# Two spectral filters and a gate: sums of the last four inverse rows on TensorE, and a new order of work

## The chip, the cores and the metric

One core of a Trainium2 chip runs the whole kernel. The metric is the device time of one execution in microseconds (us), as the median of several runs. The profile is of one execution; its span, from the first to the last instruction of the program, is a little shorter than the device time of that same execution.

## The reference

```python
# x: 2048 x 1024 (bf16), w_r, w_i: 2048 x 513 for each of A and B, gate_w: 1024
g = sigmoid((x * gate_w).sum(-1, keepdims=True))
a = irfft2(rfft2(x) * (A_w_r + 1j * A_w_i))      # over both axes, then bf16
b = irfft2(rfft2(x) * (B_w_r + 1j * B_w_i))
out = g * a + (1 - g) * b
```

Only `A_x` is used. The Fourier transforms run over the 2048 rows (s) and the 1024 columns (d) of one image.

## The kernel before

Row s = 16p + n of x lies on partition p, so the image is 16 slabs n of 128 x 1024. The work runs in stages, each a set of small tasks; a task is one entry of a list.

1. **Forward s, first radix** (`fold`, `fod`, `s1.n.t`, `evz`; n = 0 to 7 stands for a pair of slabs, t = 0 for the even and 1 for the odd columns of the d spectrum). VectorE (DVE) first folds x: sums (t = 0) or differences (t = 1) of the two halves of d, in two instructions `fold n.t.0` and `fold n.t.1`, the second of which reads backwards, so that the result lies folded for the next step. For t = 0 two further instructions `fod n.0.k` form sums and differences of that once more. Then TensorE (PE) multiplies with the cosines and sines in FM (eight 256-column matmuls for one `s1`), whose negatives `neg0` to `neg3` ScalarE (ACT) makes in FM's upper half. A `raw` task (FOLD0) leaves out the two `fod` and makes PE do their sums, in longer matmuls; a FOLD2 task does the opposite for t = 1. Each result goes from PSUM to SBUF (R3) through one eviction `evz`, on ACT or DVE.
2. **Forward d** (`d0` to `d15`, `evq`): eight matmuls each, four 128-column ones that read the t = 0 results and four 256-column ones that read t = 1; every `d` waits for all sixteen `evz`. The evictions write the RING buffer; `qc` copies two columns out for the Nyquist column.
3. **Forward s, second radix** (`s2.j.c`, `evx`), **product** with A's and B's weights (`p b.j.t`, on DVE, optionally followed by `ps`, which adds the two halves so that PE needs half the matmuls: SUMS), **inverse s** (`i b.T`, `evv`). The Nyquist column goes apart: `x5` on PE, `x5e`, then `p5.b` on GpSimd (POOL), `v5.b` on PE, `v5e.b`, and a small DMA `vf b` that needs all `evv b.*` and `v5e.b`. TensorE's list places `v5.0` and `v5.1` between the `i` tasks.
4. **Inverse d** (`dinv b.n`, `evd`; 32 of them). A `dinv0` needs all of V of filter A and `vf0`, a `dinv1` all of B and `vf1`.
5. **Inverse s, last step with the gate** (`s1i m`, m = 0 to 15, `evo`): four 512-column matmuls, weighted with RA and RB, which hold the gated cosines. The evicted cosine and sine sums are then unfolded on DVE in three steps of two instructions each: `q a/b`, `h a/b`, `y a/b`, for two slabs at a time (the last two slabs alone), and `out n` on SyncE's DMA queue (SP) writes the result. The gate's own path is `gj`, `g8`, `g9` (POOL), `grow`, `gzr`, `gzt`, `gzg`, `gmix`, `sig`, `ra`, `rb`.

The order of work is written out by hand: `ORDER` is a list of `task:engine+buffers`, `place` assigns engine and buffer from it, and each engine's instructions run in exactly that order. `:p0` to `:p3` is the PSUM slot (four of 1024 fp32 columns), `:a` ACT, `:d` DVE, `:g` POOL, `:s` SP. DMAs are all issued by SP, in list order, so a load that has to wait holds up those behind it. The loads of weights (`w b.t.c.pm`, 128 KB in each of two DMAs, mostly) keep three in flight: each waits until the third before it has landed.

All engines record through helpers, so that the profile's lines are those of helpers: L421 is the matmul, L424 a DVE or POOL tensor_tensor, L428 the ACT eviction, L429 the DVE eviction, L444 the loads and L1018 the stores. The profile names tiles without numbers: R stands for R1 to R5.

Of the kernel before, what the change touches and what calls it, by code (L numbers as in the profile page):

```python
# [6 lines left out]
ALU = mybir.AluOpType  # L7
# [14 lines left out]
mz:g x2:s x12:s table:a warm:p0 F:s x0:s x14:s x8:s x4:s w0.0.0.0:s fold1.0.0:d0 fold1.0.1:d0 fold1.1.0:d1 RM:s  # L22
fold1.1.1:d1 DM:s fold6.0.0:d2 fod1.1.1:d fod1.1.0:d fold6.0.1:d2 w0.0.1.0:s fold6.1.0:d3 fod1.0.0:d neg0:a
fold6.1.1:d3 neg1:a w0.0.0.1:s fod1.0.1:d fod6.1.0:d fod6.1.1:d s1.1.1:p1 fod6.0.0:d neg3:a fod6.0.1:d fold0.1.1:d1
s1.6.1:p2 evz1.1:a fold0.0.0:d0 SK:s fold0.0.1:d0 s1.1.0:p3 fold0.1.0:d1 neg2:a fod0.0.1:d fod0.0.0:d fold7.1.0:d3
fod0.1.1:d fod0.1.0:d evz6.1:a fold7.1.1:d3 s1.6.0:p0 fold7.0.0:d2 fold7.0.1:d2 s1.0.0:p1 fod7.1.0:d evz6.0:a
fod7.1.1:d fold4.0.0:d4 evz1.0:a fold4.1.1:d5 s1.7.1:p2 fold4.1.0:d5 evz0.0:a s1.0.1:p0 fold4.0.1:d4 fod4.1.1:d
fod4.1.0:d fod5.1.1:d fod5.1.0:d s1.4.1:p3 fold2.1.0:d0 evz0.1:a fold2.1.1:d0 s1.5.1:p1 evz4.1:a fod4.0.0:d fod3.1.0:d
fod3.1.1:d fod2.1.0:d fod2.1.1:d w0.0.1.1:s s1.3.1:p0 fold2.0.0:d3 evz5.1:a fod4.0.1:d s1.2.1:p3 evz7.1:a fod7.0.1:d
fod7.0.0:d s1.5.0:p1 fold2.0.1:d3 evz2.1:a s1.4.0:p2 fod2.0.0:d evz5.0:a fod2.0.1:d s1.7.0:p3 w0.4.0.1:s evz4.0:a  # L30
evz3.1:d s1.2.0:p1 evz7.0:a w0.4.0.0:s s1.3.0:p2 evz2.0:d evz3.0:a w0.4.1.0:s d7:p00 d2:p31 evq7:d w0.8.0.0:s d3:p11
evq2:a d6:p20 evq3:d w0.4.1.1:s d1:p02 evq6:a d0:p32 evq1:d qc1:a qc3:a w0.8.0.1:s s2.3.1:p1 evq0:a s2.3.0:p2 evx3.1:d
s2.1.1:p0 GW:s evx3.0:a s2.1.0:p3 w0.8.1.1:s evx1.1:d evx1.0:a d4:p10 d5:p20 w0.8.1.0:s evq4:a p0.3.1:d0 d10:p31
evq5:a p0.3.0:d0 s2.0.0:p0 w0.12.0.0:s ps0.3.1:d d11:p11 evq10:a qc2:d evx0.0:d s2.2.1:p2 ps0.3.0:d evq11:a s2.0.1:p3
evx2.1:d evx0.1:a s2.2.0:p0 s2.5.1:p1 qc0:a p0.0.0:d1 evx5.1:a i0.6:p3 i0.7:p2 evx2.0:d evv0.6:a w0.12.1.0:s ps0.0.0:d
s2.5.0:p1 evv0.7:a p0.0.1:d1 gj:p3 d12:p00 w0.12.0.1:s evx5.0:a d8:p22 qc5:d g8:d ps0.0.1:d p0.1.1:d0 g9:g d13:p30
evq12:a w0.12.1.1:s i0.0:p1 p0.1.0:d0 evq13:a ps0.1.1:d i0.1:p0 w1.0.0.1:s evq8:a evv0.0:d ps0.1.0:d s2.6.1:p3
evv0.1:a s2.6.0:p2 qc6:d p0.2.1:d1 w1.0.0.0:s d14:p11 evx6.1:a d9:p02 p0.2.0:d1 GS:s evx6.0:a w1.0.1.0:s i0.2:p3
evq9:a ps0.2.1:d d15:p21 w1.4.0.0:s ps0.2.0:d evq14:a evv0.2:d i0.3:p0 evq15:a w1.0.1.1:s i0.5:p1 p0.5.0:d0 i0.4:p3
evv0.3:a s2.7.0:p2 qc4:d evv0.4:a p0.6.0:d1 w1.4.0.1:s ps0.5.0:d grow:p0 evv0.5:a qc7:d p0.6.1:d1 ps0.6.0:d w1.4.1.1:s  # L40
evx7.0:a s2.7.1:p3 gzr:d s2.4.1:p1 ps0.6.1:d evx7.1:a w1.4.1.0:s s2.4.0:p2 p0.5.1:d0 gzt:p0 evx4.1:a DI:s i0.12:p3
p0.7.0:d2 ps0.5.1:d evx4.0:a w1.8.0.0:s i0.13:p1 gzg:d evv0.12:a p0.7.1:d2 ps0.7.0:d x5:p2 i0.10:p0 x5e:a evv0.13:a
p0.4.1:d1 p5.0:g ps0.7.1:d i0.11:p3 w1.8.0.1:s evv0.10:a p0.4.0:d1 ps0.4.1:d gmix0:p2 evv0.11:a w1.8.1.0:s gmix1:p1
p1.0.0:d0 ps0.4.0:d i0.15:p0 sig0:a w1.8.1.1:s i0.14:p3 p1.0.1:d0 sig1:a ps1.0.0:d i0.8:p2 evv0.15:a p1.2.1:d2
ps1.0.1:d w1.12.0.0:s v5.0:p1 evv0.14:a p1.2.0:d2 i0.9:p0 ps1.2.1:d evv0.8:a w1.12.0.1:s i1.0:p3 p1.1.0:d1 ps1.2.0:d
v5e.0:a i1.1:p2 w1.12.1.0:s evv0.9:a p1.1.1:d1 ps1.1.0:d i1.4:p1 evv1.1:a w1.12.1.1:s p1.5.1:d0 ps1.1.1:d i1.5:p0
evv1.0:a vf0:s p1.5.0:d0 i1.2:p2 ps1.5.1:d evv1.4:a i1.3:p3 p1.4.1:d2 evv1.2:a ps1.5.0:d i1.11:p1 evv1.5:a p1.4.0:d2
ps1.4.1:d i1.10:p2 evv1.3:a p5.1:g p1.6.1:d1 ps1.4.0:d i1.9:p0 evv1.11:a p1.6.0:d1 i1.8:p3 ps1.6.1:d evv1.10:a
dinv0.7:p1 p1.7.0:d0 evv1.9:a ps1.6.0:d dinv0.10:p2 evd0.7:a p1.7.1:d0 dinv0.8:p0 ps1.7.0:d evv1.8:a i1.13:p1
p1.3.0:d2 ps1.7.1:d evd0.10:a i1.12:p3 p1.3.1:d2 evv1.13:a i1.14:p2 ps1.3.0:d evd0.8:a i1.15:p1 ps1.3.1:d evv1.12:a  # L50
evv1.14:d i1.7:p0 evv1.15:a i1.6:p3 evv1.7:d v5.1:p2 evv1.6:a dinv0.12:p1 v5e.1:d dinv0.2:p0 evd0.12:a ra1:d
dinv0.0:p3 vf1:s dinv0.11:p2 rb1:d evd0.0:a evd0.2:d dinv0.6:p1 evd0.11:a dinv0.9:p3 evd0.6:d dinv0.15:p0 evd0.9:a
dinv1.8:p2 evd0.15:d dinv1.9:p1 evd1.8:a dinv1.7:p3 ra0:d evd1.9:a dinv1.6:p0 rb0:d s1i8:p20 evd1.7:d evd1.6:a
s1i9:p10 evo8.0:d dinv1.3:p0 evo9.0:a dinv1.15:p3 evd1.3:a q8a:d dinv1.11:p2 q8b:d s1i6:p11 evd1.15:a h8a:d0 h8b:d0
dinv1.10:p0 evd1.11:a s1i7:p31 y8b:d0 evd1.10:a evo6.0:d s1i15:p22 evo7.0:a dinv1.1:p0 y8a:d0 evo15.0:a q6b:d
s1i10:p13 evd1.1:a evo15.1:d dinv1.2:p3 q6a:d evo10.0:a q15a:d q15b:d dinv1.0:p2 h6b:d1 evd1.2:a s1i11:p03 h6a:d1
h15a:d0 evd1.0:a dinv1.13:p1 y6a:d1 dinv0.13:p3 y6b:d1 evo11.0:a dinv1.12:p2 evd1.13:d evd0.13:a dinv0.1:p0 q10a:d
# [249 lines left out]
class Task:  # L307
# [3 lines left out]
    n = 0  # L311
# [57 lines left out]
def build(nc, A_x, A_w_r, A_w_i, B_w_r, B_w_i, gate_w, out):  # L369
# [154 lines left out]
    for c in range(4):  # L524
        t = add(f"neg{c}", -1500 + c, {"act": (0.48, 0.6)}, None, [tF, tb])
        t.emit = lambda g, c=c: S.op("act", [lambda e: e.activation(ap(FM, 2048 + c * 512, [[1, 512]]), ap(FM, c * 512, [[1, 512]]),  # L526
                                                                  ACT.Copy, scale=-1.0)], ["F"], [("FN", c)])
        tN.append(t)
# [6 lines left out]
    allZ, evZ = [], []  # L535
    for Q in range(4):
        for t in range(2):

            st = Buf("st")
            folds, part = {}, {}  # L540
            for n0, n1 in (((0, 1), (1, 2)) if Q in (0, 3) else ((0, 2),)):
                fs = []
                for hv in range(2):
                    f = add(f"fold{2 * Q + n0}.{t}.{hv}", -900 + 2 * Q + n0, tt_cost(512 * (n1 - n0)), None,
                            [xt[2 * Q + i] for i in range(n0, n1)], [st])

                    def e_f(g, Q=Q, t=t, n0=n0, n1=n1, hv=hv, st=st):
                        nn, so = 2 * (n1 - n0), (4 * Q + 2 * n0) * 1024
                        o = st.i * 2048 + n0 * 1024
                        if t:  # L550
                            d = [[1024, nn], [-1 if hv else 1, 256]]
                            w, lo = ap(RING, o + hv * 256, [[512, nn], [1, 256]]), 511 * hv
                        else:
                            d = [[1024, nn], [-256, 2], [-1, 128]] if hv else [[1024, nn], [256, 2], [1, 128]]
                            w = ap(RING, o + 128 * hv, [[512, nn], [128 if hv else 384, 2], [1, 128]])
                            lo = 511 * hv
                        S.op(g, [tt(w, ap(R1, so + lo, d), ap(R1, so + 512 + lo, d), ALU.subtract if t else ALU.add)],
                             [("x", 2 * Q + i) for i in range(n0, n1)], [("st", st.i, i, hv) for i in range(n0, n1)])
                    f.emit = e_f
                    fs.append(f)  # L560
                if not t:
                    gs = []
                    for k in range(2):
                        f = add(f"fod{2 * Q + n0}.0.{k}", -900 + 2 * Q + n0, tt_cost(512 * (n1 - n0)), None, fs, [], [st])
# [12 lines left out]
                for i in range(n0, n1):  # L577
                    folds[i], part[i] = fs, n0
            for i in range(2):
# [18 lines left out]
                if not t:  # L598
                    u.alt = ("G", Q, part[i], {0: (pe_cost(872), 16), 1: (pe_cost(1735), 20)})
# [450 lines left out]
```

## Time and profile before

| | |
|---|---|
| device time, median of 11 runs | 128.88 us (126.47 to 131.11) |
| profiled execution, device time | 128.24 us |
| its span | 126.1 us |
| granted TensorE clock, mean | 0.974 |
| busy in the span: DVE / PE / ACT / POOL | 111.1 / 109.9 / 105.5 / 16.6 us |
| read from memory, written | 14.77 MB, 4.19 MB |

Instruction durations overlap: a DVE eviction of 128 x 1024 takes 1.22 us, but two in a row start 1.13 us apart. For sums of work the distance from start to start (the step) is what counts, and it is read from rows in which several of a kind follow without a gap. The tasks of the list appear in each engine's trace in list order, so that every DVE, ACT and PE instruction can be given its task's name by counting.

### The profile page before, as it was taken

The page shows a single profiled execution, that of the slowest core. Times are in us where ns is not written, and L with a number is a line of the kernel's source. Part 1 is how long each engine was busy: PE and PEld are TensorE (multiplying, and loading weights), DVE is VectorE, ACT ScalarE, POOL GpSimd, SP SyncE. Part 2 cuts the span into 40 slices and gives each one's busy share as a digit, 9 for nine tenths or more (in the row PEclk, how much of TensorE's full clock was granted, in tenths as well). Part 3 has the DMA queues.
Part 4 walks back from the last instruction along what each step waited for, and adds up shares of the span by engine and source line. Part 5 has one row for each costly group of instructions (what it writes and reads, how often), then busy time and mean ns, then how long its engine had stood idle before and what let it go on. Part 6 is the DMA issues. An engine that isn't in the chain of part 4 may idle for free.

```text
span 126.1 us, 4191 instructions
## 1 busy us (share of the span) xinstructions
PE 109.9 (87%) x1853; PEld 82.0 (65%) x1853; DVE 111.1 (88%) x163; ACT 105.5 (84%) x120; POOL 16.6 (13%) x22
## 2 busy tenths in 40 slices
PE   5999999699999999999499999999999999976000
PEld 2367878586468785699399889899666766631000
DVE  0699799499999999999769999999899999999940
ACT  4078999389999999999869999998799999999200
POOL 2000000000005800049749000000000000000000
PEclk9999999999999999999999999999999999999955
DMA  4999999889955759759610000000000000402997
GB/s 112 407 430 426 297 311 247 166 222 173 191 136 172 209 153 247 219 149 229 183 58 7 5 5 0 5 1 5 0 0 0 5 0 0 166 0 86 402 404 273
DMA packets 13425, 19.23 MB, mean 153 GB/s; under 512 B 2656, under 2 KB 10848, under 8 KB 13152
## 3 DMA queue, kind: packets, MB, share of 16 engines
q1 hardware_dynamic: 13408, 18.98, 49.7%
q8 instruction: 14, 0.23, 0.8%
q14 instruction: 3, 0.02, 0.0%
HBM read 14.77 MB, written 4.19 MB: 150 GB/s over the span
## 4 chain that ended last, share of the span: by engine, by line
ACT 42%; PE 19%; DVE 13%; DMA 9%; POOL 6%; issue 3%; SPq 2%; ACTq 1%; DVEq 1%
ACT R L428 34%; PE PS L421 19%; DVE RING L424 12%; DMA R<-in_A_x_dram 9%; ACT RING L428 8%; POOL P L424 6%; SPq L444 2%; DVE R L424 1%; ACTq L285 1%; DVEq L285 0%; DVEq L271 0%; ACT X L428 0%
## 5 line engine op out<-in xcount | busy, mean ns | idle before, releaser
L428 ACT ACTIVATE R<-PS 128x1024 bf16<-128x1024 f32 (+1 forms) x94 | 87.5, 1092 | 4.0 <-PE PS L421 3.5
L424 DVE TENSOR_TENSOR RING<-R 128x2048 bf16<-128x2048 bf16 (+2 forms) x74 | 59.1, 846 | 7.2 <-DMA R<-in_A_x_dram 4.9
L421 PE MATMUL PS<-DM,R 128*128 128x256 bf16 (+1 forms) x384 | 34.4, 246 | 1.2 <-ACT R L428 1.1
L421 PEld LDWEIGHTS PS<-DM,R 128*128 128x128 bf16 x384 | 28.5, 98 | 7.1 <-ACT R L428 1.8
L421 PE MATMUL PS<-SK,RING 64*128 64x128 bf16 x960 | 29.2, 217 | 0.3 <-issue 0.2
L421 PEld LDWEIGHTS PS<-SK,RING 64*128 64x128 bf16 x960 | 27.1, 102 | 2.3 <-issue 1.0
L429 DVE CAST R<-PS 128x1024 bf16<-128x1024 f32 (+1 forms) x20 | 23.4, 1190 | 0.1
L424 DVE TENSOR_TENSOR R<-R 128x512 bf16<-128x512 bf16 (+2 forms) x36 | 16.5, 508 | 1.0 <-ACT R L428 0.8
L421 PE MATMUL PS<-R,FM 128*128 128x512 bf16 x64 | 15.4, 379 | 0.9 <-ACT R L428 0.8
L428 ACT ACTIVATE RING<-PS 128x1024 bf16<-128x1024 f32 x13 | 12.6, 1055 | 1.9 <-PE PS L421 1.9
L421 PEld LDWEIGHTS PS<-R,FM 128*128 128x128 bf16 x64 | 6.0, 98 | 7.4 <-ACT R L428 2.0
L421 PE MATMUL PS<-FM,RING 128*128 128x256 bf16 (+1 forms) x66 | 8.7, 283 | 0.2 <-DVE RING L424 0.2
L424 POOL TENSOR_TENSOR P<-X,R 128x32 bf16<-128x32 bf16 x4 | 6.9, 1732 | 13.7 <-ACT X L428 11.5
L421 PE MATMUL PS<-RING,SK 64*64 64x512 bf16 (+1 forms) x128 | 8.6, 384 | 0.1
L421 PEld LDWEIGHTS PS<-FM,RING 128*128 128x128 bf16 x66 | 6.2, 98 | 2.4 <-ACT FM L526 0.6
L424 POOL TENSOR_TENSOR GW<-GW 128x8 bf16<-128x8 bf16 (+1 forms) x4 | 2.5, 666 | 38.0 <-DVE GW L429 38.0
L421 PE MATMUL PS<-R 128*128 128x512 bf16 x16 | 6.4, 588 | 1.3 <-POOL R L514 1.3
L421 PE MATMUL PS<-FM,R 128*128 128x256 bf16 (+1 forms) x64 | 7.1, 266 | 0.0
L421 PEld LDWEIGHTS PS<-FM,R 128*128 128x128 bf16 x64 | 5.9, 98 | 0.9 <-DVE R L424 0.2
L526 ACT ACTIVATE FM<-FM 128x512 bf16<-128x512 bf16 x4 | 2.3, 620 | 4.6 <-DMA FM<-c_F 4.6
L424 DVE TENSOR_TENSOR R<-RING 128x512 bf16<-128x512 bf16 (+1 forms) x12 | 5.6, 506 | 0.0
L421 PEld LDWEIGHTS PS<-R 128*128 128x128 bf16 x16 | 2.2, 143 | 5.0 <-issue 3.6
(35 smaller groups left out, 36.0 us busy)
## 6 DMA issues: line engine op xcount, KB each, us to landing
out_dram<-RING SPq DMA_DIRECT2D x7, 512.0 KB, 4.3
R<-in_A_x_dram SPq DMA_DIRECT2D x4, 512.0 KB, 5.2
R<-in_A_x_dram SPq DMA_DIRECT2D x2, 1024.0 KB, 10.1
R<-in_A_w_r_dram SPq DMA_DIRECT2D x15, 128.2 KB, 3.8
R<-in_A_w_i_dram SPq DMA_DIRECT2D x15, 128.2 KB, 3.7
R<-in_B_w_r_dram SPq DMA_DIRECT2D x15, 128.2 KB, 3.2
R<-in_B_w_i_dram SPq DMA_DIRECT2D x15, 128.2 KB, 2.8
FM<-c_F SPq DMA_DIRECT2D x1, 512.0 KB, 5.2
```

What stands on the lines that cost most here:

```text
L285: with nc.Block() as block:
L421: return lambda e: e.matmul(o, l, r, start=start, stop=stop, skip_group_check=True)
L424: return lambda e: e.tensor_tensor(out=o, in0=a, in1=b, op=op)
L428: return lambda e: e.activation(o, i, ACT.Copy)
L429: return lambda e: e.tensor_copy(o, i)
L444: t.emit = lambda g: S.op(eng, [lambda e, d=d, s=s: e.dma_start(d, s, **kw) for d, s in pairs], reads, writes, dma=kind, after=after)
L526: t.emit = lambda g, c=c: S.op("act", [lambda e: e.activation(ap(FM, 2048 + c * 512, [[1, 512]]), ap(FM, c * 512, [[1, 512]]), ACT.Copy, s ...
```

## The change

- **Last four rows.** LATE = 4: for m = 12 to 15 PE forms, besides each 512-column matmul, the folded second half with two 256-column matmuls more (12 instead of 4 matmuls in a task), using negated copies of RA and RB (`nr0`, `nr1`, 512 columns each, into RM). For these rows DVE does `q` and `y` only; their `h` are gone.
- **Folds in one instruction.** For t = 0 the two half-length folds become one full-length instruction (`fold n.0.2`) that leaves the result unfolded, and `fod` reads its second operand backwards. The raw task moves from n = 0 to n = 7; FOLD2 is empty, so `s1.7.1` is an ordinary one and its two `fod` are gone. `ps` is used for three j (A: 3 and 5, B: 6) in place of two.
- **Forward d in two parts.** `d g.0` holds the four 128-column matmuls and waits for the t = 0 evictions, `d g.1` the four 256-column ones and waits for t = 1; one eviction serves both.
- **A new list.** `neg3` and `nr0` go to DVE as tensor_scalar. Of the evictions, DVE takes 2 `evz`, 5 `evq`, 3 `evx`, 3 `evv`, 8 `evd`, 1 `evo` (before: 2, 3, 5, 4, 6, and two and a half `evo`), and all eight `qc`.

The list by engine, where the text below needs it:

```
SP   x12 F x14 x2 x0 x8 x4 w0.0.0.1 DM w0.0.0.0 GW SK w0.0.1.0 w0.0.1.1 ... w1.4.1.0 RM w1.8.0.0 w1.8.0.1
     w1.4.1.1 w1.8.1.1 w1.12.0.0 w1.8.1.0 DI vf0 w1.12.1.1 w1.12.0.1 GS w1.12.1.0 vf1 out6 out8 out10 out4
     out2 out0 out12 out14 out15
PE   ... s1.2.0 s1.3.0 d0.1 d2.1 d3.1 d3.0 gj d2.0 d0.0 d10.1 ... i1.15 i1.14 v5.1 i1.11 i1.13 i1.12 gmix1
     ... s1i11 s1i10 s1i12 dinv1.14 dinv0.14 s1i13 dinv0.15 s1i14 s1i15
DVE  fold6.0.2 fold6.1.1 fold6.1.0 neg3 ... evz4.0 evz2.0 g8 evq2 ... p1.4.0 p1.5.1 p1.5.0 p1.7.0 p1.7.1 p1.6.1 p1.6.0
     ... y0a y10a y10b q12b q12a y0b y12b q14a q14b y12a y14b y14a q15a q15b y15b y15a
ACT  ... evz5.0 evz3.0 evq3 evq0 ... evo12 evd0.14 evd1.14 evo13 evd0.15 evo14.0 evo14.1 evo15.1 evo15.0
```

Before, SP's list began `x2 x12 F x0 x14 x8 x4 w0.0.0.0 RM DM w0.0.1.0 w0.0.0.1 SK`, had GW after w0.8.0.1, vf0 after all of w1.12, and ended `out10 out0 out15 out8 out2 out12 out6 out14 out4`. DVE's list ended `y2a q14a q14b y2b h14a h14b q4a q4b y14a h4a h4b y14b y4a y4b`, PE's `dinv0.4 s1i14 s1i4 s1i5`.

The diff, cut to its core:

```diff
-SUMS = {(0, 2): 1, (1, 3): 1}
-FOLD2 = {(7, 1): 1}
-FOLD0 = {(0, 0): 1}
+SUMS = {(0, 3): 1, (0, 5): 1, (1, 6): 1}
+FOLD2 = {}
+FOLD0 = {(3, 1): 1}
-GROUPS, HALVES = [2] * 7 + [1, 1], 2
+GROUPS, HALVES, LATE = [2] * 7 + [1, 1], 2, 4
...
+        def e_n(g, c=c):
+            o, i = ap(FM, 2048 + c * 512, [[1, 512]]), ap(FM, c * 512, [[1, 512]])
+            if g == "act":
+                f = lambda e: e.activation(o, i, ACT.Copy, scale=-1.0)
+            else:
+                f = lambda e: e.tensor_scalar(out=o, in0=i, scalar1=-1.0, scalar2=None, op0=ALU.mult)
+            S.op(g, [f], ["F"], [("FN", c)])
...
+                        if hv == 2:
+                            d, w, lo = [[1024, nn], [1, 512]], ap(RING, o, [[512, nn], [1, 512]]), 0
...
+                            a = (ap(R4, w, [[512, nn], [128, 2], [1, 128]]), ap(RING, o, [[512, nn], [256, 2], [1, 128]]),
+                                 ap(RING, o + 511, [[512, nn], [-256, 2], [-1, 128]]))
...
-            u = add(f"d{g}", due("d", j), pe_cost(664), None, evZ + [tDM], [sl, qb], [], "full")
+            us = [add(f"d{g}.{t}", due("d", j), pe_cost((224, 440)[t]), None, evZs[t] + [tDM], [sl, qb], [], "full", ni=8) for t in range(2)]
...
-                    for k in range(2):
+                    for k in range(0 if t else 2):
                         fns.append(mm(ps(sl, c * 512 + k * 256, [[1, 128]]), z((k, 3 - k)[c]), ap(DM, (2 * c + k) * 128, [[1, 128]]), True, True))
-                    for h in range(2):
+                    for h in range(2 if t else 0):
                         fns.append(mm(ps(sl, c * 512 + 128, [[256, 2], [1, 128]]), z(5 - c + 2 * h),
                                       ap(DM, 512 + c * 512 + h * 256, [[1, 256]]), h == 0, h == 1))
-                S.op("pe", fns, allZ + ["DM"], [pk(sl)])
+                S.op("pe", fns, [z for z in allZ if z[2] == t] + ["DM"], [("psh", sl.i, t)], after=[pk(sl)])
...
+                if late:
+                    for c in range(2):
+                        for b, t in ((0, R3), (1, R4)):
+                            x = m * 1024
+                            w = ap(RM, b * LATE * 128 + (m - 16 + LATE) * 128, [[1, 128]]) if c else ap(FM, b * 2048 + m * 128, [[1, 128]])
+                            fns.append(mm(ps(sl, c * 512, [[1, 512]]), ap(FM, b * 2048 + m * 128, [[1, 128]]),
+                                          ap(t, x + 511 * c, [[-1 if c else 1, 512]]), b == 0, False))
...
+                            fns.append(mm(ps(sl, c * 512, [[1, 256]]), w, hi, False, False))
+                            fns.append(mm(ps(sl, c * 512 + 256, [[1, 256]]), w, lo, False, b == 1))
...
-        h0 = add(f"h{n}a", pr, tt_cost(512 * nn), None, [q0, q1], [hb], [ob])
-        h1 = add(f"h{n}b", pr, tt_cost(512 * nn), None, [q0, q1], [hb], [ob])
+        if not late:
+            hs = [add(f"h{n}{k}", pr, tt_cost(512 * nn), None, [q0, q1], [hb], [ob]) for k in "ab"]
```

## The prediction, made before the changed kernel ran

> **What bounds the kernel now.** I read the busy times, then busy time by stage, then the waits, then the chain at its end. First the page, then three stretches (first s radix; forward d up to the filter A inverse; the rest). Columns: stretch, length, busy time of PE, PEld, DVE, ACT, POOL.
>
> ```profile
> PE 109.9 (87%) x1853; PEld 82.0 (65%) x1853; DVE 111.1 (88%) x163; ACT 105.5 (84%) x120; POOL 16.6 (13%) x22
> ```
>
> ```profile
> 7.50:22.70 15.20, 15.00 (x131) 11.99 (x130) 14.40 (x29) 13.89 (x16) 0.00 (x0) 1.00 1.06 331
> 23.80:62.50 38.70, 36.65 (x827) 27.26 (x828) 37.17 (x41) 36.67 (x43) 11.48 (x13) 1.00 0.74 186
> 62.50:116.00 53.50, 52.01 (x880) 40.60 (x880) 50.72 (x73) 50.32 (x57) 4.41 (x4) 1.00 0.05 18
> ```
>
> Three engines are near their limit everywhere after 7.5 us, so no single wait carries the time: a gain must come from work removed on all three, from common stalls, or from the ends. The waits show two common stalls and a queue:
>
> ```profile
> ACT RING L428 <- PE PS L421: 1.9, 2, 1.6
> DVE RING L424 <- PE PS L421: 1.9, 1, 1.9
> PE PS L421 <- POOL P L424: 1.9, 1, 1.9
> SPq L1018 <- DVE R L424: 25.3, 2, 24.7
> ```
>
> The first is the border to forward d: `evz3.0` ends at 23.77, `d7` starts at 23.82, DVE's first `evq` at 24.70, ACT's at 25.36. The next two are one stall at 62.4: PE's list stands at `v5.0`, which waits for `p5.0` on POOL. The last is SP: finished results wait in its list behind `out0`. The chain in order of time shows stall and end:
>
> ```profile
> 55.31 7.08 POOL P L424 x4
> ...
> 113.29 3.24 ACT R L428 x4
> 116.53 0.93 ACTq L285
> 117.46 0.02 issue
> 117.48 0.37 DVE R L424
> ...
> 120.72 0.60 DVE RING L424
> ```
>
> After the last eviction (117.46) DVE works 3.86 us more, to 121.32. Then only stores run. Rows by the microsecond (last two columns: DMA share, GB/s):
>
> ```profile
> 115.00:116.00 1.00, 0.73 (x4) 0.11 (x2) 1.00 (x4) 1.00 (x3) 0.00 (x0) 1.00 0.07 29
> ...
> 118.00:121.00 3.00, 0.00 (x0) 0.00 (x0) 3.00 (x7) 0.00 (x0) 0.00 (x0) 0.76 1.02 405
> 121.00:124.00 3.00, 0.00 (x0) 0.00 (x0) 0.32 (x1) 0.00 (x0) 0.00 (x0) 0.50 1.02 401
> ```
>
> From `out0`'s issue at 115.11 eight stores (3.67 MB) drain at 403 GB/s: 9.1 us, and 1.9 us for start, landing and the end make 126.1. **The end is a drain**, not DVE's last instruction alone.
>
> **Steps used**, from start to start, from rows without a gap:
>
> ```profile
> 12.94 0.61 PE L421 MATMUL PS<-FM,R 128*128 128x128 bf16 x8
> 28.57 2.35 DVE L429 CAST R<-PS 128x1024 bf16<-128x1024 f32 x2
> 30.84 2.35 DVE L424 TENSOR_TENSOR RING<-R 128x2048 bf16<-128x2048 bf16 x2
> 111.92 0.76 DVE L424 TENSOR_TENSOR R<-R 128x512 bf16<-128x512 bf16 x2 [0.21 <-ACT R L428]
> 118.49 1.29 DVE L424 TENSOR_TENSOR R<-R 128x1024 bf16<-128x1024 bf16 x2
> ```
>
> Two casts in 2.35 with 1.22 for the last: step 1.13; products 1.13; tensor_tensor 0.34 (512) and 0.605 (1024); ACT eviction 0.91 (8 in 7.33 on the chain). PE: `dinv` 0.66, `s1i` and eight-matmul `s1` 0.87, `i` 0.89 or 0.45 with `ps`, a 128-column matmul 0.056.
>
> **Part 1, up to forward d.** Folding in one instruction saves one fixed cost per group, 2 x 0.34 - 0.605 = 0.07 (five groups, 0.35), and two `fod` of `s1.7.1` go (0.7). `neg3` on DVE is in no row: above, a 512 tensor_tensor (0.42); below, half of that, since one input is read, not two; I take 0.3. None of it reaches the path: the stretch 7.5 to 22.7 is PE's (15.0 of 15.2). The warm-up matmuls end at 7.5 in both, and PE then has fifteen tasks of 0.87 and a raw one of 1.73, 14.8 us, so `s1.3.0` ends at 22.4 (before 22.71). DVE's last fold, 19.7 by the sum from x4's landing at 14.9, is early enough. At the border `d0.1, d2.1, d3.1` (3 x 0.44) run beside `evz3.0`, except that `d3.1` needs the slot that `evz2.0` on DVE frees at about 23.1. Then `d3.0` at 23.7, ACT's first `evq` at 24.0 (before 25.36: **-1.35**), DVE's at 24.45 (before 24.70: **-0.25**). PE is 1.3 ahead in work.
>
> This needs SK and GW by 24.0 (`gj` stands ahead of `d2.0`). Here a rule speaks against the list: the Trainium skill, "DMA: Bandwidth & Descriptors" (Specifications), has transfers under 512 B run below line rate, and GW is 1024 runs of 2 B, now ahead of SK. The rows:
>
> ```profile
> 29.00:30.00 1.00, 0.96 (x19) 0.39 (x12) 1.00 (x2) 1.00 (x3) 0.00 (x0) 1.00 0.91 228
> 30.00:31.00 1.00, 1.00 (x15) 0.93 (x14) 1.00 (x2) 1.00 (x3) 0.00 (x0) 1.00 0.89 91
> ```
>
> ```profile
> GW<-in_gate_w_dram SPq DMA_DIRECT2D x1, 2.0 KB, 5.2
> ```
>
> By the rows GW took some 0.13 MB from its neighbours, 0.6 us; by the rule, counting each run as 512 B, 0.52 MB or 1.3 us (an estimate). SK landed at 23.34; RM and one weight load (0.77 MB, 1.9 us) no longer precede it, so it lands at 22.0 or 22.7, both in time. Were GW's whole 5.2 us added, 26.6, PE would stand 2.5 us: that end goes into the range.
>
> **Part 2, the work from the first `evq` on.**
> - DVE: six `h` go, 2 x 0.605 + 4 x 0.34 = 2.57; `evx` -2 and `evv` -1, 3.4; `evo` -1.7; `v5e.1` -0.3. Added: `evq` and `evd` 4 x 1.13 = 4.5; two `ps` 1.2; three `qc` 0.25; `nr0` 0.3. Net **-1.7**.
> - ACT: full evictions balance; +0.5 a half `evo`, +0.6 `v5e`, +0.5 `nr1`, -0.4 `qc`. Net **+1.2**.
> - PE: late rows 4 x 8 matmuls of 256 columns at 0.109, **+3.5**; two `i` tasks at half, -0.9; 1.3 already done. Net **+1.3**.
>
> **Part 3, the POOL stall.** `x5` now stands some ten tasks earlier and `v5.0` behind `i0.13`, so `p5.0`'s 7 us lie beside products: **-1.9** on PE and DVE, -1.7 on ACT. What is late next: `vf0` stands in SP's list ahead of three weight loads and GS. It waits for `evv0.6`, by ACT's sum at about 61.5; behind it `w1.12.1.0` is issued at 65 and lands at about 68.5. `p1.7.0` needs it at 72: hidden. `p5.1` needs it too: 68.5 + 7.1 = 75.6, while PE reaches `v5.1` at about 75 (`i1.14` follows `p1.7.1`). I put **+0.5** on PE. If `vf0` slips, all of it shows there.
>
> **Sum.** DVE: 121.32 - 0.25 - 1.7 - 1.9 = 117.4. ACT: 117.45 - 1.35 + 1.2 - 1.7 = 115.6, then `q15`, `y15` (1.3): 116.9. PE: 115.73 - 0.1 + 1.3 - 1.9 + 0.5 = 115.5, then `evo15.1`, `evo15.0` (1.5) and 1.3: 118.3. The engines lean on each other; I take 117.8 for DVE's end. Stores: `out6` and `out8` go early; `out10`, `out4`, `out2` start together when `y10b` is done, 4.6 us of DVE steps before the end (I take 5), at 112.8. Left then: 3.15 MB / 403 GB/s = 7.8, + 1.9 = 122.5. Span -3.6. The profiled execution had 2.14 us around its span: 124.6 against 128.24. The median of the runs was 0.5% above that execution: **125.2 us**, 2.9% faster.
>
> **Rivals.**
> 1. *PE becomes the bound* (25%). The late rows put 8.9 us of PE into the last stretch from `s1i12`, and PE keeps 1.9 of idle elsewhere. For it: PE's sum ends last. Against: before, PE waited for ACT at 111 to 114. DVE's end 119.7, span 124.4, median 127.2: 1.3% faster; in four of ten such cases within 1%.
> 2. *The drain hides less than I think* (11%). PE's long tasks leave DVE gaps, so that `y10b` lies 7 us ahead of the end and only the last stores trail: span 121.2, 123.9 us. For it: four of the list's last seven stores are ready early. Against: DVE is nearly full.
> 3. *Slower: `vf0` dams SP* (6%). For it: SP's list is strict, and before nothing followed `vf0` but `vf1`. If `evv0.6` ends at 67 (before, `vf0` left at 65.24), `w1.12.1.0` lands at 74, `p5.1` ends at 81, PE stands 6 us at `v5.1` with all `dinv` behind it: span 128, about 131 us. It decides against the change from a landing later than 72. Against: the forward stages end earlier.
> 4. *The change does not do what it says* (3%): SK or GW lands late, PE stands at `gj`, and the border's gain is lost and more: about 127.8.
>
> My own sum has 55%, with 123.5 to 126.5 as its range.
>
> **Chances.** A measurement of this kernel tells about 1% from no change. Faster by over 1%: 55 + 15 + 11 = 81%; within 1%: 10 + 3 = 13%; slower: 6%. The range, 123.0 to 128.0, takes in rivals 1, 2 and 4.
>
> **What would show it.** Right: no wait of PE for POOL around 62; first `evq` on ACT near 24.0; PE busy about 3 us more from 22 on; DVE's tail after the last eviction 1.3 instead of 3.86; last stores at 400 GB/s to the end. Wrong: PE waiting for POOL at `v5.1` or for SK at `gj`; DVE idle by over 5 us after 24; `y10b` later than 114.

## The result, and the profile after

| | before | changed kernel |
|---|---|---|
| device time, median | 128.3 us (126.47 to 131.11, 47 runs, the first 11 among them) | **125.38 us** (124.44 to 126.81, 12 runs) |
| profiled execution: device time, span | 128.24, 126.1 us | 125.39, 123.6 us |
| busy DVE / PE / ACT | 111.1 / 109.9 / 105.5 us | 108.5 / 112.4 / 105.8 us |

The ratio is 0.982, with a 95% interval of 0.979 to 0.985: 1.8% faster. It compares only those executions of each kernel that lie within 1.5% of its fastest, and so differs from the quotient of the medians, 0.977. (In the profiles of two kernels below, "before with the stores in order" and "before with d in two parts", TensorE's clock was halved for 3.4 us from about 63 us on. Only what lies outside that stretch is used of them, except in the last section.)

The page's first part after the change:

```profile
PE 112.4 (91%) x1853; PEld 84.8 (69%) x1853; DVE 108.5 (88%) x155; ACT 105.8 (86%) x119; POOL 14.4 (12%) x22
```

DVE has 2.6 us less to do, PE 2.5 us more, and PE is now the fullest engine. The stretches that the prediction read, in the changed kernel (stretch, length, busy time of PE, PEld, DVE, ACT, POOL; then granted clock, DMA share, GB/s):

```profile
7.50:22.70 15.20, 15.20 (x136) 12.91 (x133) 14.59 (x26) 12.84 (x15) 0.00 (x0) 1.00 0.95 297
23.80:62.50 38.70, 37.42 (x854) 27.27 (x852) 38.37 (x44) 37.77 (x43) 6.80 (x13) 1.00 0.65 188
62.50:116.00 53.50, 52.02 (x838) 41.01 (x835) 49.92 (x72) 50.40 (x56) 6.93 (x4) 1.00 0.14 46
...
118.00:121.00 3.00, 0.00 (x0) 0.00 (x0) 0.90 (x3) 0.00 (x0) 0.00 (x0) 0.60 1.02 406
121.00:124.00 3.00, 0.00 (x0) 0.00 (x0) 0.00 (x0) 0.00 (x0) 0.00 (x0) 0.50 0.55 209
```

All three engines are busier in the middle stretch: the border and the POOL stall are out of it. From 118.93 on, when DVE ends (before: 121.32), only stores run, at 406 GB/s: the end is still a drain, 4.7 us long (before 4.8). The waits that answer to those shown before:

```profile
POOL P L426 <- DMA R<-in_B_w_i_dram: 20.3, 1, 20.3
...
DVE R L431 <- PE PS L423: 3.2, 4, 2.0
...
PE PS L423 <- POOL P L426: 1.4, 1, 1.4
```

PE still has a wait for POOL, 1.4 instead of 1.9 us, but it is another one. The chain in order of time says which:

```profile
61.19 0.60 SPq L446
...
65.66 4.02 DMA R<-in_B_w_i_dram
69.68 0.07 issue
69.75 6.75 POOL P L426 x3
...
76.82 39.68 PE PS L423 x420
```

Read upward from the end: PE runs 39.7 us without a gap from `v5.1` (76.82). `v5.1` waited for `p5.1` on POOL, that for the last weight load `w1.12.1.0` (landed 69.68), and that stood in SP's list behind `vf0`, issued at 61.19 when `evv0.6` was done. Nothing waits for POOL at 62 any more. DVE's wait of 2.0 (at `evv1.11`, to 78.4) is the same stall, seen from DVE: it comes in place of the 1.9 us that DVE stood at 62.

### The profile page after: what moved, and what is told of

The parts are those of the page before. It is cut to its first block, busy times and chain, and to the rows that moved or that the text cites. A ratio compares the mean times of both kernels' runs of the same rounds, so it can differ in the third digit from the quotient of the medians.

```text
span 123.6 us, 4183 instructions
## 1 busy us (share of the span) xinstructions
PE 112.4 (91%) x1853; PEld 84.8 (69%) x1853; DVE 108.5 (88%) x155; ACT 105.8 (86%) x119; POOL 14.4 (12%) x22
## 4 chain that ended last, share of the span: by engine, by line
PE 56%; ACT 25%; POOL 6%; DMA 3%; SPq 3%; issue 1%; DVE 1%; ACTq 0%; DVEq 0%; POOLq 0%
PE PS L423 56%; ACT R L430 17%; ACT RING L430 8%; POOL P L426 5%; DMA R<-in_B_w_i_dram 3%; SPq L446 3%; POOL R L516 0%; ACTq L287 0%; DVE RING L426 0%; DVEq L287 0%; DVE R L426 0%; POOLq L287 0%; ACT X L430 0%; POOLq L1085 0%
## 5 line engine op out<-in xcount | busy, mean ns | idle before, releaser
L430 ACT ACTIVATE R<-PS 128x1024 bf16<-128x1024 f32 (+1 forms) x97 | 90.1, 1079 | 6.5 <-PE PS L423 6.3
L423 PE MATMUL PS<-DM,R 128*128 128x128 bf16 (+1 forms) x384 | 34.2, 246 | 0.0
L431 DVE CAST R<-PS 128x1024 bf16<-128x1024 f32 x17 | 20.4, 1220 | 3.3 <-PE PS L423 3.2
L423 PE MATMUL PS<-R,FM 128*128 128x512 bf16 (+1 forms) x80 | 17.7, 358 | 0.0
L426 DVE TENSOR_TENSOR R<-R 128x512 bf16<-128x512 bf16 (+2 forms) x30 | 13.8, 508 | 0.5 <-ACT R L430 0.3
L426 POOL TENSOR_TENSOR P<-X,R 128x32 bf16<-128x32 bf16 x4 | 9.1, 2294 | 38.8 <-DMA R<-in_B_w_i_dram 20.3
L430 ACT ACTIVATE RING<-PS 128x1024 bf16<-128x1024 f32 x11 | 10.7, 1060 | 0.5 <-PE PS L423 0.5
L423 PE MATMUL PS<-FM,R 128*128 128x256 bf16 x56 | 6.6, 273 | 0.0
L431 DVE CAST RING<-PS 128x1024 bf16<-128x1024 f32 x5 | 6.1, 1222 | 0.3 <-PE PS L423 0.2
L423 PEld LDWEIGHTS PS<-RING,SK 64*64 64x64 bf16 x128 | 2.7, 105 | 4.6 <-ACT RING L430 1.7
```

The costliest lines, as they stand in the source:

```text
L423: return lambda e: e.matmul(o, l, r, start=start, stop=stop, skip_group_check=True)
L426: return lambda e: e.tensor_tensor(out=o, in0=a, in1=b, op=op)
L430: return lambda e: e.activation(o, i, ACT.Copy)
L431: return lambda e: e.tensor_copy(o, i)
```

## The experiments

Two measures are used. The times give a ratio to runs of the kernel before on the same chip; the changed kernel has 0.982 by it, and 0.1 points are about 0.13 us. The trace of one execution gives places, but x4's landing moved between 14.7 and 16.3 us from one execution to another, and all that follows moved with it; so places are counted from x4's landing or from the end of `s1.3.0`, the last task of the first stage. From the end of `s1.3.0` the changed kernel takes 101.5 us.

### Is the first stage PE's? `fold4.0.2` behind x4

In the changed kernel `s1.3.0` ends 7.04 us after x4's landing, in before 7.80. DVE's work behind x4, first in before (start, duration, engine and line, tiles and number, and the wait ahead of it):

```profile
15.01 1.29 DVE L424 TENSOR_TENSOR RING<-R 128x1024 bf16<-128x1024 bf16 x2 [0.64 <-DMA R<-in_A_x_dram]
16.22 0.68 DVE L424 TENSOR_TENSOR R<-RING 128x1024 bf16<-128x1024 bf16 x1
16.82 0.68 DVE L424 TENSOR_TENSOR RING<-R 128x1024 bf16<-128x1024 bf16 x1
17.43 1.35 DVE L424 TENSOR_TENSOR R<-RING 128x1024 bf16<-128x1024 bf16 x3
18.70 0.68 DVE L424 TENSOR_TENSOR RING<-R 128x1024 bf16<-128x1024 bf16 x1
19.42 1.29 DVE L424 TENSOR_TENSOR R<-RING 128x1024 bf16<-128x1024 bf16 x2
```

and in the changed kernel:

```profile
15.14 1.29 DVE L426 TENSOR_TENSOR RING<-R 128x1024 bf16<-128x1024 bf16 x2 [0.33 <-PE PS L423]
16.35 1.28 DVE L426 TENSOR_TENSOR R<-RING 128x1024 bf16<-128x1024 bf16 x2
17.55 1.22 DVE L426 TENSOR_TENSOR RING<-R 128x2048 bf16<-128x2048 bf16 x1
18.80 1.29 DVE L426 TENSOR_TENSOR R<-RING 128x1024 bf16<-128x1024 bf16 x2
```

Both groups begin 0.10 us after x4's landing (14.91 and 15.04); the label "PE" on the second wait names an engine that had long been done. The first group has two short operations more, in the row with x3 (17.43): `fod7.0.1` and `fod7.0.0`, 0.67 us, which the raw task took with it when it moved to n = 7. The group for x4 in one fold instead of two is 0.07 shorter. So DVE's last `fod` ends 5.06 us behind x4's landing instead of 5.80.

PE's list changed there as well. In before, seven `s1` tasks stand behind x4's first folds; in the changed kernel six, since the raw `s1.7.0` now comes ahead of them. The chains of the two kernels show PE in this stretch, first in before, then in the changed kernel, there with the warm-up (start, length, number of matmuls):

```profile
16.36 6.36 PE PS L421 x56
```

```profile
1.29 22.36 PE PS L423 x163
```

In before PE works the seven tasks off without a gap, one every 0.875 us, from 1.45 to 7.80 us behind the landing. The sixth of them, `s1.2.0`, needs DVE's last `fod`, which ends only 0.09 us ahead of its start. By these figures less work on DVE alone would have changed nothing in before. PE lost 0.87 us behind x4 and DVE 0.74; the stage gained 0.76. In the changed kernel's profile PE has no gap up to forward d, and `s1.2.0` starts 0.03 us later than PE alone would have it. In the six other kernels with the same first stage x4 landed later (15.55 us or more), and it is 0.16 us; there `s1.2.0` starts 0.06 us after the last `fod`. Is DVE's work now on the path? The test puts more of it behind x4:

```diff
-fold4.0.2 ... fold2.1.1 fold2.1.0 ...
+... fold2.1.1 fold2.1.0 fold4.0.2 ...
```

> The changed kernel, with fold4.0.2 (1.22 us on DVE) behind fold2.1.0 instead of ahead of fold2.1.1, so that it stands behind x4's landing and not ahead of it. Theory (the first stage is x4's landing and DVE's work behind it): s1.3.0 ends at x4's landing + 8.2 instead of + 7.04, PE stands about 1.1 us ahead of s1.5.0 or s1.2.0, all behind moves by that, and the time is 126.3 to 126.6. Rival (the prediction's step: the stretch is PE's, DVE's folds are early enough): no change, 125.1 to 125.7.

Measured: 127.42 us, ratio 0.994 (0.991 to 0.996). x4 landed at 16.02, `s1.3.0` ended at 24.32: +8.30. DVE's timeline shows the moved fold as third in the first row, and DVE idle ahead of it until x4 is there:

```profile
16.12 2.43 DVE L426 TENSOR_TENSOR RING<-R 128x1024 bf16<-128x1024 bf16 x3 [2.12 <-DMA R<-in_A_x_dram]
18.58 1.29 DVE L426 TENSOR_TENSOR R<-RING 128x1024 bf16<-128x1024 bf16 x2
19.79 1.22 DVE L426 TENSOR_TENSOR RING<-R 128x2048 bf16<-128x2048 bf16 x1
21.04 0.69 DVE L426 TENSOR_TENSOR R<-RING 128x1024 bf16<-128x1024 bf16 x1
```

```profile
PE PS L423 <- DVE R L426: 1.1, 2, 0.6
```

The theory holds: PE stood 1.1 us ahead of `s1.5.0` and `s1.2.0` (the two waits above), and the span counted from x4's landing grew by 1.26 (123.59 - 15.04 = 108.55 against 125.83 - 16.02 = 109.81); the ratio by 1.2 points. In the changed kernel, work added on DVE behind x4 is on the path, one for one.

### The border: both parts of `d` wait for everything again

```diff
-... evZs[t] + [tDM] ...
+... evZ + [tDM] ...
...
-... [z for z in allZ if z[2] == t] + ["DM"] ...
+... allZ + ["DM"] ...
```

The list is the same but for `d0.1`, which stands behind `evz3.0`.

> The changed kernel with both parts of each d waiting for all sixteen evz, as one d did before; the parts, their order and everything else stay. Theory (the head start of three d.1 is passed on through engines without slack): first evq on ACT at 24.9 instead of 23.65, and all of it at the end, span 124.6 to 124.9. Rival (later waits soak it up, the dam at v5.1 above all, which is set by loads and POOL): 123.6 to 124.0.

Measured: 127.51 us, ratio 0.994 (0.991 to 0.997). ACT around the border, in this kernel and then in the changed one:

```profile
23.06 1.02 ACT L430 ACTIVATE R<-PS 128x1024 bf16<-128x1024 f32 x1 [0.81 <-PE PS L423]
25.88 1.94 ACT L430 ACTIVATE RING<-PS 128x1024 bf16<-128x1024 f32 x2 [1.80 <-PE PS L423]
```

```profile
22.11 1.02 ACT L430 ACTIVATE R<-PS 128x1024 bf16<-128x1024 f32 x1 [0.42 <-PE PS L423]
23.65 3.77 ACT L430 ACTIVATE RING<-PS 128x1024 bf16<-128x1024 f32 x4 [0.51 <-PE PS L423]
```

The first row is `evz3.0`, the second the first `evq`: ACT stands 1.80 us between them instead of 0.51. The span from the end of `s1.3.0` grew by the same 1.3 us, from 101.5 to 102.8: in the trace the border's stall passes to the end whole. The ratios say 1.2 points, 1.5 us.

**Before with d in two parts** does that part alone, on the old kernel, with `d7.1` and `d2.1` ahead of `evz3.0`:

```diff
-evz2.0 ... evz3.0 ... d7 ... d2
+evz2.0 d7.1 d2.1 evz3.0 ... d7.0 d2.0
```

> The kernel before with d in two parts, d7.1 and d2.1 ahead of evz3.0, and nothing else of the change. Theory (head start of two parts, 0.9 us of PE, passed on to the end): first evq on DVE 0.4 and on ACT 0.8 earlier, span 0.5 to 0.9 shorter, 125.2 to 125.6. Rival (the border's wait is soaked up before the end): 125.9 to 126.1.

Measured: 127.55 us, ratio 0.992 (0.989 to 0.996), some 1.0 us, a little more than the 0.5 to 0.9 expected. ACT's first `evq` starts at 24.60 (x4 at 15.02) instead of 25.36 (x4 at 14.91), DVE's at 24.37 instead of 24.70.

### The last four rows: LATE back to 0

```diff
-GROUPS, HALVES, LATE = [2] * 7 + [1, 1], 2, 4
+GROUPS, HALVES, LATE = [2] * 7 + [1, 1], 2, 0
```

with `h12`, `h14` and `h15` back in DVE's list and without `nr0`, `nr1`.

> The changed kernel with the last four rows as before: four matmuls each, h12, h14, h15 back on DVE, no nr0 and nr1; nothing else moved. Theory (the end is the drain of the stores from y10b on, and y10b stays where it is since the six h come after it): PE ends 3 us earlier, DVE about 2 us later, y10b within 0.4 of 113.9, the last stores a little late; span 124.2 to 124.5 instead of 123.6, so the late rows are worth 0.6 to 0.9 us. Rival A (DVE's tail counts in full): 2.5 us worse, 126.1. Rival B (PE is the bound at the end and the late rows cost what they save): 123.6 or less.

Measured: 126.92 us, ratio 0.991 (0.989 to 0.994). DVE ended 2.9 us later counted from `s1.3.0`, but the drain began at the same place (`y10b`), so the span from `s1.3.0` grew by 0.7 only (102.2). PE ended only 0.9 us earlier, not 3 as expected: with 3.5 us of its work gone it waits 1.0 and 0.8 us for ACT's evictions ahead of its last two tasks. The times say more than the trace, 0.9 points or 1.2 us; why is open. So the late rows save 2.9 us at DVE's end, and only a part of it at the kernel's, which is the drain's.

### `vf0` and the last weights: three places for one wait

**Behind the last loads on SP:**

```diff
-vf0 w1.12.1.1 w1.12.0.1 GS w1.12.1.0 vf1
+w1.12.1.1 w1.12.0.1 w1.12.1.0 vf0 GS vf1
```

> The changed kernel with one move in SP's list: vf0 (and GS) behind the last three weight loads of B. Theory (the dam behind vf0 lies on the chain: vf0, the loads, p5.1 on POOL, v5.1, then PE without a gap to the end): the last weight load lands at about 67 instead of 69.7, PE's wait of 1.4 us for POOL at v5.1 goes, DVE's of 2.0 at evv1.11 shrinks, span 122.2 to 122.7 instead of 123.6. Rival (only another wait in its place: dinv0.3 now waits for vf0, or the engines are full anyway): the POOL wait goes, the span stays at 123.4 to 123.8.

Measured: 125.47 us, ratio 0.981 (0.976 to 0.985), no gain; 101.4 us from the end of `s1.3.0`. The weights landed at 66.85 and `v5.1` waited for nothing, but among the waits of this kernel stands a new one:

```profile
PE PS L423 <- DMA R<-V: 1.3, 1, 1.3
```

It is `dinv0.3`, which needs `vf0` (landed at 67.02). The wait changed its owner.

**On ACT's queue** (this kernel and the next are made from "stores in order", below):

```diff
-evv0.6:a ... vf0:s
+evv0.6:a vf0:a
```

> The changed kernel with the stores in order of readiness, and vf0 issued by ACT right behind evv0.6, so that neither the loads wait for vf0 nor vf0 for the loads. Theory (p5.1 holds PE at v5.1 because of the dam; with the load order alone changed the wait only moved to dinv0.3): both waits go, evv1.11 and the rest come 1.0 to 1.4 earlier than with the stores alone, span 121.1 to 121.6 against its 122.6, counted from the same landing of x4. Rival (full engines take up the slack): unchanged within 0.3.

Measured: 124.15 us, ratio 0.966 (0.962 to 0.970), against 0.9685 for the kernel it is made from. ACT's timeline:

```profile
60.16 2.09 ACT L430 ACTIVATE R<-PS 128x1024 bf16<-128x1024 f32 x2
62.28 0.56 ACTq L446 DMA_DIRECT2D R<-V  x1
63.21 3.77 ACT L430 ACTIVATE R<-PS 128x1024 bf16<-128x1024 f32 x4 [0.96 <-PE PS L423]
```

ACT has no eviction between 62.25 and 63.21, though the next one, `evv1.0`, could have started when `i1.0` ended at 62.32. Issuing one 4 KB transfer cost ACT 0.9 us, PE waited 0.9 us for the slot that was not emptied (at `i1.2`), and that `v5.1` no longer waited gained nothing.

**On POOL's queue:**

```diff
-evv0.6:a ... vf0:s
+evv0.6:a vf0:g
```

> The kernel with the stores in order of readiness, and vf0 issued by POOL's own DMA queue right behind evv0.6 instead of SP's list (GS moves with it, it stands by itself on SP). Theory: with e1 the loads were freed but vf0 was late, with e7 both were free but the issue held ACT for 1 us; POOL has nothing to do at 61 us, so here no engine pays. vf0 leaves at about 61.2 and lands at about 65, the last weights land at about 67, p5.1 starts then and ends at about 74, before PE reaches v5.1: the 1.1 to 1.4 us that PE waited there are gone, and dinv0.3 does not wait. Counted from x4's landing, DVE ends 1.0 to 1.3 us earlier than in the kernel with the stores in order, and the time is 122.6 to 122.9 us. Rival: PE, DVE and ACT are all full by then and something else is late by as much (as in e1 and e7): within 0.3 us of 123.9.

Measured: 123.82 us, ratio 0.961 (0.955 to 0.968), not to be told from the kernel it is made from. From the DMA issues (bytes each, and us from issue to landing):

```profile
R<-V POOLq DMA_DIRECT2D x1, 4.0 KB, 4.6
...
R<-V SPq DMA_DIRECT2D x1, 4.0 KB, 1.8
```

The second row is `vf1`, later and with no load near it. `vf0`, issued by POOL at 62.70 among the weight loads, took 4.6 us to land, so `dinv0.3` waited 1.07 us. The same transfer issued by ACT, in the kernel above, took as long:

```profile
R<-V ACTq DMA_DIRECT2D x1, 4.0 KB, 4.6
```

The rival is right a third time: PE loses 1.3 to 1.5 us in all between 61 and 78 wherever `vf0` goes.

### Stores in the order in which they are ready

```diff
-out6 out8 out10 out4 out2 out0 out12 out14 out15
+out2 out8 out6 out4 out10 out0 out12 out14 out15
```

each placed right behind its last `y`; `y15` goes to another buffer, so that it does not wait for `out10`.

> The changed kernel with the stores issued as soon as their rows are ready (out2 out8 out6 out4 out10 out0 out12 out14 out15 instead of out6 out8 out10 out4 out2 out0 out12 out14 out15; y15 in another buffer so that it does not wait for out10). Theory (the end is the drain of what is left at y10b): 2.1 MB are left then instead of 3.1, the drain is over soon after DVE's end, which stays at 118.9; out15 lands 2.7 after its issue; span 122.2 to 122.5. Rival (the last store's own way sets the end, whatever was queued ahead): DVE's end + 4.6, 123.6.

Measured: **123.88 us**, ratio 0.9685 (0.964 to 0.973), the simplest version that beats both kernels. The last stretches of it, and then those of the changed kernel (last column GB/s):

```profile
110.00:113.00 3.00, 3.00 (x30) 2.35 (x28) 3.00 (x7) 3.00 (x5) 0.00 (x0) 1.00 0.49 195
...
118.00:120.00 2.00, 0.00 (x0) 0.00 (x0) 1.90 (x7) 0.72 (x2) 0.00 (x0) 1.00 0.82 330
120.00:122.50 2.50, 0.00 (x0) 0.00 (x0) 0.04 (x1) 0.00 (x0) 0.00 (x0) 0.58 0.62 233
```

```profile
110.00:113.00 3.00, 3.00 (x28) 2.12 (x26) 3.00 (x6) 3.00 (x4) 0.00 (x0) 1.00 0.12 48
...
118.00:120.00 2.00, 0.00 (x0) 0.00 (x0) 0.90 (x3) 0.00 (x0) 0.00 (x0) 0.65 1.02 403
120.00:123.50 3.50, 0.00 (x0) 0.00 (x0) 0.00 (x0) 0.00 (x0) 0.00 (x0) 0.50 0.77 296
```

At 110 to 113 the changed kernel moved 48 GB/s with `out4` and `out2` finished and waiting behind `out10`; now 195. DVE ends as far from `s1.3.0` as in the changed kernel (96.83 against 96.85), but the program ends 2.5 us behind DVE instead of 4.7. So 2.2 us of the drain were the list's order. The rest is mostly the last store itself, 2.0 us from its issue (120.07) to its landing (122.09).

**The same on the kernel before:**

```diff
-out10 out0 out15 out8 out2 out12 out6 out14 out4
+out8 out6 out15 out10 out12 out0 out2 out14 out4
```

> The kernel before with its stores issued as soon as their rows are ready (out8 out6 out15 out10 out12 out0 out2 out14 out4 instead of out10 out0 out15 out8 out2 out12 out6 out14 out4), nothing else. Theory (the end is the drain of what stands behind out0 in SP's list): four stores (1.8 MB) are left from 115 on instead of eight (3.7 MB), DVE still ends at 121.3, out4 lands about 2.7 later: span 124.4 to 124.7 instead of 126.1, counted from the same landing of the x loads. Rival (DVE's end and the last store alone set it): 126.1.

Measured: 126.48 us, ratio 0.983 (0.979 to 0.988). The tail behind DVE fell from 4.8 to 3.1 us. On the old kernel this one reordering gains as much as the whole change did: the two intervals are all but the same.

### The POOL stall alone

**`v5.0` three tasks later in before** (`v5e.0` is evicted only after `i1.4` has reused its PSUM slot, so A's Nyquist column is not formed in it):

```diff
-v5.0 ... i0.9 ... i1.0 ... v5e.0 i1.1 ... i1.4 evv1.1
+i0.9 ... i1.0 ... i1.1 v5.0 ... i1.4 evv1.1 v5e.0
```

> The kernel before with v5.0 three PE tasks later (behind i0.9, i1.0, i1.1) and v5e.0 behind evv1.1, nothing else. Theory (PE's wait of 1.9 us for POOL at 62.4 and DVE's of 1.9 at p1.1.0 are one stall on the path of all three engines): both go, PE is then held by ACT's evictions alone for a task or two, the end comes 1.3 to 1.9 earlier, span 124.2 to 124.8. Rival (the stall had slack behind it, because PE, DVE and ACT catch up before the end): 0.5 or less, 125.6 to 126.1.

Measured: 128.15 us, ratio 0.996 (0.993 to 0.999). In the trace the stall is gone and DVE ends 1.3 us earlier counted from x4's landing (119.77 - 14.66 = 105.11, before 106.41); the times show 0.5. The profiled execution was the fastest of its 22 runs (126.7), which may be part of that.

**`x5` earlier in before:**

```diff
-gzt:p0 ... i0.12:p3 ... i0.13:p1 ... x5:p2 i0.10:p0 x5e
+x5:p0 gzt:p3 x5e p5.0 ... i0.12:p1 ... i0.13:p2 ... i0.10:p0
```

> The kernel before, with x5 and x5e ahead of gzt, i0.12 and i0.13, and p5.0 with them; the four tasks exchange PSUM slots, nothing else moves. Theory: p5.0 starts 1.8 us earlier (53.5) and PE's wait for POOL at v5.0 falls from 1.9 us to 0.3 or less. In the profiled executions of two of the kernels derived from before (stores in order, d in two parts) the granted clock stood at 0.50 for 3 us right behind that wait, in before's own it did not; if the wait is what sets it off, there is no drop here. DVE ends 1.4 to 1.9 us earlier counted from x4's landing (106.4 in before), the time is 126.3 to 126.9, and the runs spread less. Rival 1, from the kernel with v5.0 three tasks later, whose span fell by 1.3 in the profiled execution and whose median fell by 0.5 only: the clock falls somewhere else instead, and the time is 127.5 to 128.1. Rival 2: the forward stages give the stall back, no change within 0.3.

Measured: 127.41 us, ratio 0.996 (0.993 to 0.999). x4 landed at 16.03 and DVE ended at 121.34: 105.31 behind it, 1.10 less than before. PE's gap at `v5.0` is 0.41 instead of 1.86; DVE still stood 0.6 there. Between the theory (1.4 to 1.9) and the first rival (0.5): the stall was worth 1.1 to 1.3 in the trace and 0.4 points, about 0.6 us, in the times. The clock was not halved in this profile (1.00 from 5.7 to 118.3 us), so what makes the times smaller than the trace is not found.

### Both remaining waits at once

From "stores in order": (a) `fod4.0.1`, `fod4.0.0` ahead of x4's folds, with `s1.5.0` and `s1.4.0` ahead of `s1.2.1`; (b) `v5.1` two tasks later. In this kernel `i1.13` stands ahead of the `ps1.6.0` that it needs, so B's rows T = 13 are formed from products that are not yet summed.

```diff
-fold2.1.1 fold2.1.0 fod4.0.1 fod4.0.0 ...  s1.2.1 s1.3.1 s1.5.0 s1.4.0 ...  v5.1 i1.11 i1.13 i1.12
+fod4.0.1 fod4.0.0 fold2.1.1 fold2.1.0 ...  s1.5.0 s1.4.0 s1.2.1 s1.3.1 ...  i1.11 i1.13 v5.1 i1.12
```

> The kernel with the stores in order of readiness, and two moves: (a) fod4.0.1 and fod4.0.0 ahead of x4's folds, with s1.5.0 and s1.4.0 ahead of s1.2.1 and s1.3.1 on PE and evz3.1 on DVE in place of evz4.0; (b) i1.11 and i1.13 ahead of v5.1, so that PE has two tasks more while POOL works on p5.1. Theory: (a) DVE waited 1.0 us for x4 in that kernel's profile with 1.2 us of fod left to do, so s1.3.0 ends at x4's landing + 6.3 to 6.5 where x4 lands after 16, and about 22 otherwise; (b) the 1.1 us of PE at v5.1 are gone, with nothing behind it late, since vf1 needs evv1.12 anyhow, which comes later. Together 1.2 to 1.8 us: 122.1 to 122.7. Rival: (b) moves the wait to another place, as the three moves of vf0 did, and only (a) is gained: 123.2 to 123.5.

Measured: 123.32 us, ratio 0.962 (0.956 to 0.968), the rival's time. For (a), x4 landed early here (14.89), `s1.3.0` ended at +6.77 and PE had no gap above 0.1 us from its first `s1` on: the stage is PE's then, and only 0.27 is gained. For (b), PE does not wait at `v5.1`, but waits 0.3 and 0.5 us at the next two tasks, and the span from `s1.3.0` is only 0.27 shorter than in the kernel it is made from (99.07 against 99.34). DVE has a new wait:

```profile
76.67 0.69 DVE L427 TENSOR_TENSOR RING<-RING 128x1024 bf16<-128x1024 bf16 x1 [1.33 <-PE PS L424]
```

That is `ps1.6.0`, and it waits because `i1.13` stands ahead of it. So (b) is not settled: the next wait here is one that the list itself made.

## Why the prediction was right, and where it was not

It said 125.2 us and 2.9% faster; 125.38 us and 1.8% were measured. Direction and range held; the gain was put too high, in the profile too, where the span fell by 2.5 us and not by 3.6. The steps, one by one:

- **Part 1, "None of it reaches the path": wrong.** The stretch was read as PE's since PE was busy for 15.0 of 15.2 us, and PE's work was summed from the end of the warm-up. In the profiled execution that sum came close (7.04 to 22.08; 7.5 to 22.4 was put). What it left out is that PE's last tasks wait for x4 and for DVE's work behind it: `s1.3.0` ends 7.80 us after x4 in five executions of kernels with the old folds, 7.04 in seven with the new, wherever between 6.4 and 7.7 the warm-up ended, and added DVE work moved it one for one. Two sums met within 0.2 us there. Both became shorter behind x4, DVE's by fewer folds and PE's by the moved raw task: worth 0.76 us.
- **The border: right.** Counted from `s1.3.0`, ACT's first `evq` comes 1.08 us earlier (1.57 against 2.65), DVE's 0.17; -1.35 and -0.25 were put. The absolute places (23.65 and 23.90 against 24.0 and 24.45) are earlier by the 0.3 that part 1 had left out, DVE's by another 0.2. The undone border costs 1.3 us in the trace.
- **SK with GW ahead of it: no cost.** SK landed at 20.41, before either value of the prediction (22.0 by the row, 22.7 by the rule of the Trainium skill, "DMA: Bandwidth & Descriptors", Specifications), and nothing waited for it. This does not test the rule, since the loads taken from in front of SK are an estimate too. In the other kernels with the new list SK landed at 21.5 to 23.0, with a later x4, and PE did not wait either.
- **Part 2: right in size.** From the end of `s1.3.0` on DVE is busy for 91.8 instead of 93.5 us (-1.7 was put), ACT for 90.4 instead of 89.5 (+1.2), PE for 91.6 instead of 88.7 (+1.3 was put, which is +2.6 with the 1.3 "already done" that fall behind `s1.3.0` too). `v5e.1`, put at 0.3, was 0.7 us long on DVE in before. `neg3` on DVE took 0.29 us; 0.3 was put. DVE's tail behind the last eviction is 1.3 us, as predicted.
- **Part 3: the mechanism right, two terms mis-sized.** The stall at 62 went and `v5.1` is the next one late; PE's wait for POOL there, which the prediction listed as a sign of being wrong, did appear. "+0.5 on PE" measured 1.38: `w1.12.1.0` landed at 69.68, not 68.5, and PE resumed at 76.82, not 75.5. From there PE needed 39.7 us to its end, 40.0 by the prediction's figures, so most of the 1.0 us by which PE's end was missed is that wait. The -1.9 for the old stall was too much as well: alone it gave 1.1 to 1.3 in the traces and 0.5 to 0.6 in the times. On DVE it gave nothing net: its end, counted from `s1.3.0`, moved by 1.76 (98.61 to 96.85), which is its work alone, where -0.25, -1.7 and -1.9 were summed. One stall of 1.9 us went, and one of 2.0 us came.
- **The sum's choice.** Of 117.4, 116.9 and 118.3, 117.8 was taken; DVE ended at 118.93. PE's sum, the last of the three, was the nearest, and from `v5.1` on PE runs 39.7 us without a gap. That speaks for rival 1's mechanism, PE as the bound, at a smaller size than its 119.7, but it is not shown: without the late rows' 3.5 us PE ended only 0.9 us earlier, and `y10b`, with which the drain begins, did not move.
- **The drain: right.** `y10b` ended 5.0 us ahead of DVE's end (5 was put), at 113.93, and 113.93 + 7.8 + 1.9 = 123.6 is the span measured.
- **The frame around it: wrong twice, the other way.** 1.8 us lay around the span, not 2.14, and the median of 47 runs of before (128.3) is that of its profiled execution, not 0.5% above it. These two, 0.3 and 0.6 us, took back most of the span's 1.1 us error. That was luck: the time came out closer than the steps deserve, while the gain did not.

Rival 2 did not come to pass by the change, since its list kept `out4` and `out2` behind `out10`. The reordered stores then gave the end that it described, by another way: `y10b` stayed 5.0 us ahead of DVE's end, but less was left to drain. Rival 3 did not come near: `vf0` left SP at 61.19, not at 67. Rival 4's late SK did not occur.

## What to carry to other kernels

Where an engine is 99% busy in a stretch, still sum the work behind the last load on the other engines: two sums can end within 0.2 us of each other, and then work has to go from both. A strictly ordered DMA queue is a schedule of its own: write its entries in order of readiness first, since on this kernel that alone gave as much as the whole change. When a wait is moved three times and returns each time under another name, suspect that the engines around it are full, and look for work to remove; that this would gain something here was not tried.

## What the runs showed of the hardware that was not expected

- **The first loads vary.** x4's landing lay between 14.66 and 16.29 us in fourteen profiled executions, with the loads ahead of it unchanged within each kernel family, and the first stage's end moved with it.
- **A small DMA takes longer among loads.** 4 KB within SBUF landed 1.7 to 1.8 us after its issue with no load near it (`vf1`, from SP). Among the weight loads `vf0` took 2.4 to 3.9 us from SP's queue and 4.6 from ACT's as well as from POOL's. Issued by ACT it cost ACT 0.9 us of evictions. Whether the queue itself or only the loads in flight beside it make the 4.6 is not shown.
- **The clock can halve behind a stall.** In the profiled execution of "before with the stores in order" (third from last: granted clock):

```profile
61.00:62.00 1.00, 0.00 (x0) 0.00 (x0) 1.00 (x2) 1.00 (x3) 1.00 (x2) 1.00 0.77 228
62.00:63.00 1.00, 0.11 (x7) 0.14 (x8) 0.50 (x1) 0.84 (x1) 0.74 (x2) 0.97 0.77 184
63.00:66.00 3.00, 3.00 (x74) 2.95 (x73) 0.62 (x1) 1.37 (x2) 0.83 (x4) 0.50 0.11 35
66.00:67.00 1.00, 1.00 (x34) 1.00 (x32) 1.00 (x2) 0.40 (x1) 0.00 (x0) 0.82 0.00 0
```

Behind PE's wait for POOL the clock stood at 0.50 for 3.4 us, and the way from `v5.0` to the end of `i1.1` took 4.8 us instead of 3.4. The same was seen in "before with d in two parts" (3.4 us at 0.50, and 5.1 for the way), and not in before's own execution with the same wait, nor in the two kernels in which the wait was gone or short, nor behind the waits of 0.9 to 1.4 us in the changed kernel and those made from it. The half rate and its length go with the Trainium skill, "TensorE: Matmul & The Clock Gate" (Part 1), by which the clock is gated to half in windows of 3.4 us that run freely. But the page asks for at least one idle window, and PE was idle here for only 1.97 us (1.77 in the other kernel; 1.86 in before, without effect). So half rate followed on shorter gaps here, and what sets it off is open.
